# Two spectral filters on one core: the inverse transforms by halves of the columns instead of by branches

## The chip, the cores and the metric

One core of a Trainium2 chip. The metric is device time in microseconds, of the core from start to end of one execution. Engines: TensorE (PE) multiplies matrices into PSUM; VectorE (DVE) and ScalarE (ACT) do elementwise work and move results out of PSUM ("evictions"); SyncE (SP) and GpSimd (POOL) here only issue DMA transfers, which all run on the same 16 DMA engines. Each engine works through its own instruction queue in order and waits on semaphores.

## What is computed

Two branches, A and B, filter the same input `x` (2048 x 1024, bf16) in the frequency domain with different complex weights (2048 x 513), and a gate by row mixes them:

```
g = sigmoid((x * gate_w).sum(-1, keepdims=True))
a = irfft2(rfft2(x) * (A_w_r + 1j * A_w_i)).astype(bf16)
b = irfft2(rfft2(x) * (B_w_r + 1j * B_w_i)).astype(bf16)
return g * a + (1 - g) * b
```

The forward transform is needed once, the product and the inverse twice.

## The kernel before

**The steps.** The 2048-point transform along the rows is split into 128 x 16 points, the 1024-point one along the columns is done by multiplications with cosine and sine tables after folding.

1. `x` comes in 8 transfers. VectorE folds (`fS`, `fT`, for three of eight also `f2`), TensorE does the 128-point transform (`stage_s1`, table F), evictions `Z` write it.
2. `stage_d`: the column transform with table DM, 16 groups of 8 matmuls 128 x 256, evictions `Q`. `stage_s2`: the 16-point transform with table SK, 8 groups of 16 matmuls (64 x 64 tiles, 512 columns), evictions `X` into R4. R4 then holds the spectrum in 16 slots of 2 x 513 elements; four slots are one slot group `sq`.
3. `prod(b, m)`: VectorE multiplies spectrum and weights of branch `b`, two instructions of 2052 elements each, so four for each branch and slot group.
4. `stage_i1(b, m)`: the 16-point inverse of a slot group `sq = m // 2` and half `th = m % 2` of the output rows, 64 matmuls with 64 x 32 tiles and 512 columns (32 wide ones of 64 x 64 in two units). Two evictions `V` of 1024 elements (by ScalarE mostly) bring it to a ring of 28 cells of 512 elements in SBUF.
5. `turn`: a transfer from SBUF to SBUF moves the ring's cells to other partitions, 128 KB each, 64 of them, half on SP and half on POOL. A cell is free again when its turn has landed.
6. `s1inv`: the 128-point inverse for each of 16 row phases n2 and two column kinds c, 8 matmuls 128 x 128 with the gate's tables FM and DM, which sum the two branches (eviction `G`); then `Di`, the column inverse, 4 matmuls 128 x 256 with table DI (eviction `o`). VectorE adds and subtracts (`e`, `y`), SP stores (`out`).

The gate comes from Z (`gate_row`), and `gates`, `gmix` make the tables FM and DM from the table RM (`sig`, `RA`, `RB`).

**The order.** All 16 units of branch A come first, then those of B. While A's products and units run, B's weights arrive: they go to the place where x was (R1), A's to a place of their own (R5). Weights come as rows of 513 elements; one `wpart` transfer is 4 rows for 32 partitions, 128.2 KB (some of A's are twice that), half of them on SP and half on POOL. The tables RM and DI are loaded late, behind given units of B.

**The planner.** Every step is a node with a cost for each engine it may run on. `Plan.run` simulates the engines with these costs and ranks given in RANK and ENGS, places tiles in PSUM banks and ring cells, and writes down the order in which nodes start. `Sched` then fills each engine's queue in that order and adds the semaphore waits. Nothing is reordered on the chip.

The lines that an instruction shows in the profile are mostly those of helpers: L503 every matmul, L506 every elementwise operation of two tensors, L528 ScalarE's and L529 VectorE's evictions, L538 every transfer. They are told apart by tiles and shapes: `R<-R 128x2052` is a product, `64*32 64x512` the 16-point inverse, `DM,R` with 256 columns D, `FM,R` and `DM,R` with 128 columns the 128-point inverse, `DI,RING` Di, `RING<-PS 128x1024` after 46 us V, `R<-RING` a turn.

Of the kernel before, what the change touches and what calls it, by code (L numbers as in the profile page):

```python
# [2 lines left out]

# [10 lines left out]
NS = 513  # L14
# [4 lines left out]
WSPLIT = (((0, 4), (4, 8), (8, 16)), ((0, 4), (4, 8), (8, 12), (12, 16)))  # L19
RANK = (  # L20
    "9v8j0d0e0f0g0h0i0j0k0l0m2z0n0o0p0q0r0s0t0u0v0w0x0y0z1011121314151617191a1c1d1ebacafgey61dzc23u3j3d3p3v4t5r4q4f514j63al5v"
    "4x6s5i7db2686u9q70a7bf6f8vbj95c4bw7g4a7jaucnbkdgbz9s9yaxbledcketc1ewf4fbe6f9enfi3l8h3c6nbp9x7qdyas9mezfcej3a3y54625x6g6c"
    "6v36e33b6a3x3zan4o4z6k6w7275797p82833nef43cu6t6xdu717rcd8acz8od19add9l45eh58eo7u86eq8m8wdtb0dxbee8d7f0dh5jfed5f2c9cfffcm"
    "cq1g1h1i1j1k1l1m1n1o1p1q1r1t1u1v1w1x1y1z212223242527292a2b2c2d2e2f3w46474p37343i39353m3o383t404s4i4d55595g5s5w494k4h564l"
    "4r5a4u4w5b6e5e5p6h64656b6j5d5f6m7b667c7e5q898l7y8b9e8k6l6o6p6r6z8q9n8y8u9r9d789o9w9tara3a67l7n7o7s7vata4awa880b3abb5aj2j"
    "7x818x9088c7b9ccbc98aqb6bm9ccibxd3cb2kbvcjfafh9fdccsdkd49kdmd8drd9aoe5dvege4a9adaz33bhepebereuaeagbyc0c3cwdfdodwe2e7e9fj"
    "fkbdapbue0elei5y2u968t9994f7fl06090003320b02072n043r1s081f4g2l0a2t0501202p1b532m18316d2w263s412g7t3q2o4b7z442q4e280c2r74"
    "2h855o2s4m8d5t2v4v4c3f8f5u2x4y8i5z3057422y5n762i91603e5k977h3h5l525c9i7i3k699z87676y484n777m3ga18p6i73av936q7f7w5hbg9j8c"
    "7kbi9p8n848z507a9ga0bqak8s8ebrb19h8rah8gbtbo9u9bc6cpa2ay925mafb7aic8d0acb4cedbb8bnbsaactdichcod6e1cxcra5bbcgcvamdnevdedj"
    "d2eaecf1dqdpc5clcyfmf3ekf5emdseeexfdf8fof6dldaesfnfp")  # L30
ENGS = (
    "-------------------------------------------------a-a---a-a---a-a---a-a---a-a-----a-a-----a-a-----d-a-a--d--d--a---a-d-d-"
    "a--d-da-da-d-a-d-a--d-da-da-a-d-d-a--a-aa-aa-a-d-a-a--a-aa-aa-------------------------------------a--d---a--d-------a--a"
# [4 lines left out]
UNITS = ((0, 0), (0, 1), (1, 0), (2, 0), (3, 0), (1, 1), (2, 1), (3, 1))  # L38
TD = 3
PAIRS = {"warm": 12, "S2": 16, "I1": 64, "I1w": 32, "S25": 8, "gate": 8, "zg": 4, "gm": 4, "S1i": 8, "S1a": 4, "S1b": 4, "Di": 4}  # L40
WLATE = 1
BLAG = 6
WEARLY = 3
WIDE = 2
# [938 lines left out]
```

## Time and profile before

| | us |
|---|---|
| median of 3 runs | 128.88 (128.09 to 129.44) |
| profiled execution, first to last instruction | 131.6 |
| x load, folding, 128-point transform | 0 to 22.9 |
| D and S2 | 22.9 to about 46 |
| products and 16-point inverse, VectorE full | 46 to 80.4 |
| last units of branch B, gate tables | 80.4 to 96.8 |
| 128-point inverse, Di, outputs | 96.8 to 131.6 |

The profile gives one execution's span, 2.7 us above the median of the runs shown. Its rows are counted from its start. A group's row shows its count, busy time, the mean of one instruction, and the idle time just ahead of it with what ended it; because neighbouring instructions overlap, busy time divided by count is a little less than the mean of one.

### The profile page before, as it was taken

The page shows a single profiled execution, that of the slowest core. Times are in us where ns is not written, and L with a number is a line of the kernel's source. Part 1 is how long each engine was busy: PE and PEld are TensorE (multiplying, and loading weights), DVE is VectorE, ACT ScalarE, POOL GpSimd, SP SyncE. Part 2 cuts the span into 40 slices and gives each one's busy share as a digit, 9 for nine tenths or more (in the row PEclk, how much of TensorE's full clock was granted, in tenths as well). Part 3 has the DMA queues.
Part 4 walks back from the last instruction along what each step waited for, and adds up shares of the span by engine and source line. Part 5 has one row for each costly group of instructions (what it writes and reads, how often), then busy time and mean ns, then how long its engine had stood idle before and what let it go on. Part 6 is the DMA issues. An engine that isn't in the chain of part 4 may idle for free.

```text
span 131.6 us, 4299 instructions
## 1 busy us (share of the span) xinstructions
PE 106.7 (81%) x1844; PEld 72.8 (55%) x1844; DVE 105.3 (80%) x156; ACT 96.5 (73%) x129; POOL 33.8 (26%) x66
## 2 busy tenths in 40 slices
PE   6699995999999797997885640886799999999940
PEld 2288863976777353333332310443369989999820
DVE  1379998487889999999999994024469899999992
ACT  4399998477877997995972922671567869999960
POOL 0000999980000005051441410120334420000000
PEclk9999999999999999999999999599589999999998
DMA  4999999999999999757665890364439560348464
GB/s 99 398 421 413 399 238 240 240 222 194 230 239 235 228 245 234 195 145 210 181 183 173 213 289 24 85 177 149 148 93 263 178 207 0 159 173 345 173 249 183
DMA packets 14021, 27.87 MB, mean 212 GB/s; under 512 B 2577, under 2 KB 8721, under 8 KB 13874
## 3 DMA queue, kind: packets, MB, share of 16 engines
q1 hardware_dynamic: 10720, 19.18, 47.3%
q0 software_dynamic: 3136, 8.40, 25.3%
q8 instruction: 14, 0.23, 0.8%
q14 instruction: 5, 0.04, 0.1%
q10 hardware_dynamic: 146, 0.02, 0.1%
HBM read 15.01 MB, written 4.19 MB: 146 GB/s over the span
## 4 chain that ended last, share of the span: by engine, by line
PE 33%; DMA 26%; DVE 21%; ACT 11%; issue 6%; SPq 1%; DVEq 0%; ACTq 0%; POOL 0%; POOLq 0%
PE PS L503 33%; DMA R<-RING 22%; DVE RING L506 11%; ACT RING L528 7%; DVE R L506 6%; DMA R<-in_A_x_dram 4%; ACT R L528 4%; DVE RING L529 2%; DVE R L529 1%; SPq L538 1%; DVE FM L529 0%; ACT FM L858 0%; DVEq L244 0%; ACTq L244 0%; POOL R L538 0%
## 5 line engine op out<-in xcount | busy, mean ns | idle before, releaser
L528 ACT ACTIVATE RING<-PS 128x1024 bf16<-128x1024 f32 (+1 forms) x62 | 53.4, 920 | 25.7 <-PE PS L503 16.1
L506 DVE TENSOR_TENSOR R<-R 128x2052 bf16<-128x2052 bf16 (+2 forms) x68 | 49.3, 779 | 0.3
L503 PE MATMUL PS<-R,SK 64*32 64x512 bf16 (+1 forms) x960 | 33.5, 409 | 14.1 <-ACT RING L528 11.5
L528 ACT ACTIVATE R<-PS 128x1024 bf16<-128x1024 f32 (+2 forms) x55 | 41.4, 839 | 1.1 <-PE PS L503 1.0
L503 PE MATMUL PS<-DM,R 128*128 128x256 bf16 (+1 forms) x256 | 32.0, 247 | 1.0 <-ACT R L528 1.0
L538 POOL DMA_DIRECT2D R<-RING x32 | 17.3, 541 | 60.0 <-DMA R<-RING 24.0
L503 PEld LDWEIGHTS PS<-R,SK 64*32 64x32 bf16 (+1 forms) x960 | 15.0, 99 | 31.7 <-issue 13.2
L529 DVE CAST RING<-PS 128x1024 bf16<-128x1024 f32 (+1 forms) x18 | 19.2, 1079 | 12.6 <-PE PS L503 12.5
L503 PEld LDWEIGHTS PS<-DM,R 128*128 128x128 bf16 x256 | 25.9, 106 | 3.8 <-ACT R L528 1.5
L506 DVE TENSOR_TENSOR RING<-R 128x1024 bf16<-128x1024 bf16 (+1 forms) x34 | 21.2, 654 | 5.3 <-DMA R<-in_A_x_dram 5.0
L503 PE MATMUL PS<-DI,RING 128*128 128x256 bf16 x128 | 17.2, 273 | 0.3 <-ACT RING L528 0.3
L503 PE MATMUL PS<-FM,R 128*128 128x128 bf16 x128 | 16.5, 219 | 0.2 <-ACT FM L858 0.2
L503 PE MATMUL PS<-R,RING 128*128 128x256 bf16 (+1 forms) x128 | 12.3, 253 | 1.8 <-ACT R L611 1.3
L503 PEld LDWEIGHTS PS<-FM,R 128*128 128x128 bf16 x128 | 12.4, 98 | 1.0 <-ACT FM L858 0.4
L503 PEld LDWEIGHTS PS<-R,RING 128*128 128x128 bf16 x128 | 10.3, 98 | 4.6 <-ACT R L611 1.8
L529 DVE CAST R<-PS 128x512 bf16<-128x512 f32 (+2 forms) x13 | 10.5, 816 | 2.6 <-PE PS L503 2.5
L503 PEld LDWEIGHTS PS<-DI,RING 128*128 128x128 bf16 x128 | 11.5, 98 | 1.7 <-ACT RING L528 0.7
L503 PE MATMUL PS<-RING,SK 64*64 64x512 bf16 (+2 forms) x160 | 9.4, 340 | 1.0 <-ACT R L528 0.6
L538 POOL DMA_DIRECT2D R<-in_A_w_r_dram x6 | 3.6, 600 | 12.4 <-DMA R<-in_A_x_dram 12.4
L503 PEld LDWEIGHTS PS<-RING,SK 64*64 64x64 bf16 (+1 forms) x160 | 3.9, 107 | 4.9 <-ACT R L528 1.3
L538 POOL DMA_DIRECT2D R<-in_B_w_i_dram x9 | 5.6, 634 | 0.0
L538 POOL DMA_DIRECT2D R<-in_B_w_r_dram x8 | 5.2, 646 | 0.0
(30 smaller groups left out, 35.2 us busy)
## 6 DMA issues: line engine op xcount, KB each, us to landing
R<-in_A_x_dram SPq DMA_DIRECT2D x8, 512.0 KB, 7.8
R<-RING SPq DMA_DIRECT2D x32, 128.0 KB, 3.9
R<-RING POOLq DMA_DIRECT2D x32, 128.0 KB, 3.5
out_dram<-RING SPq DMA_DIRECT2D x7, 512.0 KB, 2.6
R<-in_B_w_i_dram SPq DMA_DIRECT2D x8, 128.2 KB, 21.5
R<-in_B_w_r_dram POOLq DMA_DIRECT2D x8, 128.2 KB, 17.1
R<-in_B_w_r_dram SPq DMA_DIRECT2D x7, 128.2 KB, 20.9
R<-in_B_w_i_dram POOLq DMA_DIRECT2D x7, 128.2 KB, 17.8
```

What stands on the lines that cost most here:

```text
L503: return lambda e: e.matmul(o, l, r, start=start, stop=stop, skip_group_check=True)
L506: return lambda e: e.tensor_tensor(out=o, in0=a, in1=b, op=op)
L528: return [lambda e: e.activation(o, i, ACT.Copy)]
L529: return [lambda e: e.tensor_copy(o, i)]
L538: lambda e: [lambda q, d=d, s=s: q.dma_start(d, s) for d, s in pairs()],
```

## The change

**Halves.** The columns 0 to 511 are split in half H (256 to 511, done first) and half L (0 to 255); column 512 is done by itself. A product instruction covers one half, one branch and one slot group, and four slots instead of two (2048 elements). A unit of the 16-point inverse covers one half of *both* branches side by side (512 columns), so the units are named I1H or I1L with slot group and th, as in I1H2.1. Its two V evictions fill two cells each, and one turn moves 256 KB in rows of 1024 elements: 32 turns, TH and TL. Column 512 has four small products (`mul5`), 72 tiny matmuls (`I5`), and 2 matmuls in each L unit that add it with a unit matrix.

**The 128-point inverse of H** (`S1H`, evictions `GH` of 1024 into the place of the used spectrum) needs only H turns and stands between L units in TensorE's queue. Only that of L (`S1L`, `GL`) is left for the end. `Di2` then takes both column kinds, its eviction is 1024 long, `e` too; the last two row phases are done singly (`Di`).

**Places.** Weights of A and B and x share one array, WAB. Products overwrite weights; H's first products stand in the second half of TV, where the L turns land, so L turns wait for the last H unit. `o` and `e` stand in WAB where products of slot groups 0 and 1 were.

**Loads.** RM and DI come early, and weights piece by piece for both branches.

**Order.** The planner is gone: ORDER, ENGS and CELLS hold the order, the engine of each node and the place of each tile, and `replay` reads them. Written out by name, the queues around the change are (WA3.100 is A's weights of slot group 3, odd 1, c 0, J 0; mulH3A0 is half H, slot group 3, branch A, first of two instructions):

```
SP:   x14 F x6 x0 x4 x10 x2 WA3.100 x12 x8 WA2.011 DM WA3.111 WA2.111 WA1.111 WA0.111 DI SK
      WA2.000 WA1.000 WA0.000 RM WA3.000 WA3.011 WA2.100 WA1.011 WA1.100 WB2.100 WB2.011 WB3.111
      WB2.000 WB2.111 WB3.011 WB3.000 WB3.100 WB1.100 WB1.111 WB0.000 WA0.011 WB1.011 WB0.111
      WA0.100 WB1.000 WB0.100 WB0.011 TH2.10 TH2.00 TH3.00 TH3.10 TH1.00 TH1.10 TH0.10 TL2.10
      TL2.00 TH0.00 TL1.10 TL1.00 TL3.10 TL0.10 TL0.00 TL3.00, then the stores
PE:   ... D3.3 D3.2 D2.3 D3.1 D3.0 D2.2 S2.3.1 D2.0 D2.1 gm0 S2.3.0 S2.2.0 S2.2.1 D0.0 D0.1 D0.2
      gm1 D0.3 D1.1 D1.2 S2.0.1 D1.0 D1.3 I1H2.1 I1H2.0 S2.1.1 S2.1.0 I1H3.0 I1H3.1 I5 S2.0.0
      I1L2.1 I1H1.0 I1H1.1 I1L2.0 I1H0.1 I1H0.0 I1L1.1 I1L1.0 I1L3.1 S1H10 S1H14 S1H8 S1H2
      I1L0.1 I1L0.0 S1H4 S1H12 I1L3.0 S1L13 S1L12 S1L10 S1L11 Di2.13 ... S1H0 ... S1H6 ... Di15.0
DVE:  ... Q3.3 Q3.2 Q3.0 X3.11 Q2.1 X3.00 RA0 mulH3A0 X2.11 mulH3A1 Q0.1 mulH2A0 Q0.3 mulH2B0
      mulH2A1 mulH2B1 RB0 RA1 mulH3B0 RB1 mulH3B1 VH2.00 mulL2A0 mulL2B0 mul5 mulL2A1 mul5 mulL2B1
      mul5 mul5 mulH1B0 mulH1A0 mulH1B1 mulH1A1 mulL3A0 mulL3B0 mulH0B0 mulH0A0 mulH0B1 mulH0A1
      mulL1B0 mulL1A0 mulL1B1 mulL1A1 mulL3A1 mulL0B0 mulL3B1 mulL0B1 mulL0A0 VL1.00 VL3.10 mulL0A1
      GH8 GH2 VL0.10 VL0.01 GH12 VL3.00 GL12 o12 e12 ... y15
```

POOL's queue has the other 32 weight transfers and the other 16 turns. The diff, cut to its core:

```diff
-WSPLIT = (((0, 4), (4, 8), (8, 16)), ((0, 4), (4, 8), (8, 12), (12, 16)))
-RANK = (
...
+HL = (256, 0)
+TL = (0, 16384)
+PIECES = ((0, 4), (4, 8), (8, 12), (12, 16))
...
+    def replay(self, order, engs, spots):
...
+            n.eng = names[e]
...
+                    t.at = int(next(spots), 36)
...
+    WAB = sb("WAB", 4 * WH)
+    TV = sb("TV", 32768)
...
+             {"ps": ("ps", 4), "p1": ("ps", 8), "st": ("ring", 4), "q": ("ring", 2), "qx": ("ring", 2), "v": ("ring", 14),
+              "gt": ("ring", 5), "o": ("late", 8), "e": ("late", 8), "y": ("ring", 5), "w": ("ring", 1)})
...
+    cload("sp", RM, 0, "RM", 0, 2048, ["RM"])
...
+    for ci in range(4):
+        for b in range(2):
+            for odd in range(2):
+                for c in range(2):
+                    for J in range(2):
+                        wpart(b, ci, J, odd, c)
+    P.key = ("in", 1)
+    cload("sp", DI, 0, "DI", 0, 2048, ["DI"], more=["xg"])
...
+    def ploc(lh, b, o, cx, s):
+        if o:
+            return WAB, b * 2 * WH + (1 - cx) * WH + s * WP + HL[lh]
+        if lh:
+            return WAB, b * 2 * WH + cx * WH + s * WP + 256
+        return TV, TL[1] + b * 8192 + s * 512 + cx * 256
+
+    def prod(lh, b, sq):
+        P.key = ("P", lh, b, sq)
+        l0 = HL[lh]
+        s0 = 4 * sq
+        x = ap(R4, s0 * 2 * NS + l0, [[2 * NS, 4], [NS, 2], [1, 256]])
+        r = [("X", s0 + i, c, 1 - lh) for i in range(4) for c in range(2)] + wkeys(b, sq)
         for o in range(2):
...
+            P.add("mul", vt(2048), lambda e, w=w, d=d: [tt(d, x, w, ALU.mult)], r, [("P", lh, b, sq, o)], after=old)
...
+                            T, off = ploc(lh, 0, pr // 2, pr % 2, 4 * sq + a + 2 * i)
+                            bs = ploc(lh, 1, pr // 2, pr % 2, 4 * sq + a + 2 * i)[1] - off
...
-                                            rp(b, ps[a], (i * 4 + pr) * NS + c, [[1, 512]], 64 * j, 64), pr == 0, pr == 3))
+                                            ap(T, off, [[bs, 2], [1, 256]], 64 * j, 64), pr == 0, pr == 3))
...
+        old = [("P", 0, b, q, 0) for b in range(2) for q in range(4)] if lh else allz
...
+            ev("V", 1024, lambda j=j: (rg(v[j], 0, [[256, 2], [512, 2], [1, 256]]), psl(t[j], 0, [[512, 2], [256, 2], [1, 256]])),
+               [(t[j],)], [(v[j], 0, 2)], alloc=[v[j]])
+            dma("turn", ("sp", "pool")[j], lambda j=j: [(AP(TV, (64 * j + sq) * pt + TL[lh] + th * 8192, [[4 * pt, 16], [1024, 8], [1, 1024]]),
+                                                         rg(v[j], 0, [[1, 1024]]))], 0.262, 118, [(v[j], 0, 2)], [("V", lh, sq, th, j)], after=old)
...
+    for n2 in range(0, 16, 2):
+        P.key = ("SH", n2)
+        t = Tile("ps", 2)
+        pe("S1H", [128] * 16, lambda n2=n2, t=t: s1inv(0, n2, t, 0) + s1inv(0, n2 + 1, t, 1), vkeys(0, n2), [(t,)], alloc=[t])
+        ev("GH", 1024, lambda n2=n2, t=t: (ap(R4, 2 * n2 * NS + 256, [[NS, 4], [1, 256]]), psl(t, 0, [[256, 4], [1, 256]])),
+           [(t,)], [("GH", n2), ("GH", n2 + 1)], after=[("X", n2 + r, c, 1) for r in range(2) for c in range(2)])
...
+            pe("S1L", [128] * 8, lambda n2=n2, t=t: s1inv(1, n2, t, 0), vkeys(1, n2), [(t,)], alloc=[t])
+            ev("GL", 512, lambda g=g, t=t: (rg(g, 0, [[1, 512]]), psl(t, 0, [[1, 512]])), [(t,)], [(g, 0, 1)], alloc=[g])
...
+                pe("Di2", [256] * 8, both, [(g, 0, 1), ("GH", n2), "DI"], [(t,)], alloc=[t])
+                ev("o", 1024, lambda r=r, t=t: (rg(o, r * 1024, [[1, 1024]]), psl(t, 0, [[1, 1024]])), [(t,)], [(o, 2 * r, 2 * r + 2)],
+                   alloc=[o] if r == 0 else [], after=oldw)
...
+    P.replay(ORDER, ENGS, CELLS)
```

More of the change, by code (lines that the diff above doesn't have):

```diff
@@ L789, in stage_i1 @@
+    def stage_i1(lh, sq, th):
+        P.key = ("I", lh, sq, th)
+        v = [Tile("v", 2), Tile("v", 2)]
         t = [Tile("ps", 2), Tile("ps", 2)]
+        pk = [("P", lh, b, sq, o) for b in range(2) for o in range(2)]
         def fns():
```

532 lines of the change are left out of this document (188 added, 344 removed), and 3 rows, old and new, of the table P.

## The prediction

> **What bounds the kernel now.** I read the table of stretches first, then the chain of waits, then the groups and the transfers. All times are of one profiled execution, counted from its start; its span and its engines' totals:
>
> ```profile
> span 131.6 us, 4299 instructions
> ...
> PE 106.7 (81%) x1844; PEld 72.8 (55%) x1844; DVE 105.3 (80%) x156; ACT 96.5 (73%) x129; POOL 33.8 (26%) x66
> ```
>
> The stretches (busy us and instructions of each engine, granted clock, DMA share, GB/s):
>
> ```profile
> core 0: us, PE busy (x) PEld busy (x) DVE busy (x) ACT busy (x) POOL busy (x), PEclk, DMA share, GB/s
> 22.90:46.10 23.20, 22.24 (x260) 16.58 (x260) 18.89 (x22) 17.63 (x18) 6.36 (x12) 1.00 1.06 227
> 46.10:80.40 34.30, 24.98 (x744) 11.51 (x744) 34.23 (x31) 24.23 (x26) 9.86 (x18) 1.00 0.75 199
> 80.40:96.80 16.40, 11.59 (x272) 5.39 (x273) 4.34 (x7) 7.99 (x10) 2.96 (x6) 0.79 0.39 116
> 96.80:125.20 28.40, 27.94 (x380) 25.75 (x377) 27.43 (x59) 25.85 (x52) 4.43 (x9) 1.00 0.54 185
> 125.20:131.60 6.40, 1.19 (x10) 0.62 (x8) 3.90 (x13) 1.99 (x5) 0.00 (x0) 0.90 0.53 212
> ```
>
> Four stages have four limits. From 22.9 TensorE is full with the forward transforms (D, S2) while the DMA engines are full with weights. From 46.1 VectorE is full with the products (34.23 of 34.30). From 80.4 nothing is full: 16.4 us with VectorE busy for 4.34. From 96.8 three engines are nearly full together. The third stage is the loose one; its rows in the chain (start, us, what), with the last operation, and in the timeline:
>
> ```profile
> 74.45 7.04 DMA R<-RING
> ...
> 128.71 0.42 DVE RING L506
> ```
>
> ```profile
> 81.52 2.85 ACT L528 ACTIVATE RING<-PS 128x1024 bf16<-128x1024 f32 x3 [4.86 <-DMA R<-RING]
> 82.68 5.25 PE L503 MATMUL PS<-R,SK 64*32 64x512 bf16 x128 [5.38 <-ACT RING L528]
> ...
> 88.00 1.23 DVE L529 CAST RING<-PS 128x1024 bf16<-128x1024 f32 x1 [7.64 <-PE PS L503]
> ...
> 88.35 1.93 PE L503 MATMUL PS<-R,SK 64*32 64x512 bf16 x64 [0.42 <-ACT RING L528]
> ...
> 92.94 3.50 PE L503 MATMUL PS<-R,SK 64*32 64x512 bf16 x64 [2.11 <-ACT RING L528]
> ```
>
> A turn issued at 74.45 lands 7.04 us later, ScalarE waits for its buffer, TensorE for ScalarE, and VectorE, out of products, for TensorE. After the idle 5.38 us the granted clock is low, and a 16-point unit of 64 matmuls takes 3.50 where the undisturbed one takes 1.93. The last VectorE operation ends at 129.1; the last store then needs 2.5.
>
> **The change part by part.** By the numbers of operations little goes. Products stay 32 of (now) 2048 elements, plus four of 32. The 16-point inverse stays 16 units. Two of them, of 32 wide matmuls, become 64 narrow ones; and column 512 gets 72 tiny matmuls and 16 additions:
>
> ```profile
> 40.45 0.29 PE L503 MATMUL PS<-RING,SK 128*64 128x2 bf16 x8
> ...
> 46.14 3.96 PE L503 MATMUL PS<-R,SK 64*64 64x512 bf16 x64 [0.86 <-DVE R L506]
> ```
>
> The two wide units take 3.96, 1.98 each, so the 1.93 of a narrow one changes nothing. At 0.29/8 = 0.036 the 72 tiny ones take 2.6 us of TensorE, covered by VectorE's products. 64 turns of 128 KB become 32 of 256 KB, the same bytes. The 128-point inverse keeps its 256 matmuls, of which 96 move ahead of the tail. Evictions there change from 64 of 512 to 22 of 1024 and 20 of 512, the same elements. So the gain can only be in idle time: the 16.4 us stage, which gets the H columns' 128-point inverse as work while turns are under way.
>
> What must be paid is in the loads. Now A's products run while B's weights still arrive; after, the first 16-point unit needs A's and B's weights of slot group 2. Product H2B0 (the fourth mul in VectorE's order) waits for SP's 19th weight transfer, and everything behind it on VectorE waits too. How fast weights come: five issues from the timeline, then the same five among the transfers (KB, us from issue to landing), then the stretch in which x comes:
>
> ```profile
> 6.25 0.58 SPq L538 DMA_DIRECT2D R<-in_A_w_r_dram  x1
> 14.03 0.87 SPq L538 DMA_DIRECT2D R<-in_A_w_i_dram  x1
> 28.56 0.70 POOL L538 DMA_DIRECT2D R<-in_B_w_i_dram  x1
> 30.02 2.22 SPq L538 DMA_DIRECT2D R<-in_B_w_r_dram  x1
> 41.14 1.76 SPq L538 DMA_DIRECT2D R<-in_B_w_i_dram  x1
> ```
>
> ```profile
> R<-in_A_w_r_dram SPq DMA_DIRECT2D x1, 128.2 KB, 12.6
> R<-in_A_w_i_dram SPq DMA_DIRECT2D x1, 256.5 KB, 29.0
> R<-in_B_w_i_dram POOLq DMA_DIRECT2D x1, 128.2 KB, 19.4
> R<-in_B_w_r_dram SPq DMA_DIRECT2D x1, 128.2 KB, 20.9
> R<-in_B_w_i_dram SPq DMA_DIRECT2D x1, 128.2 KB, 14.1
> ```
>
> ```profile
> 8.00:12.00 4.00, 4.00 (x43) 3.39 (x41) 3.94 (x7) 4.00 (x6) 0.00 (x0) 1.00 1.04 420
> ```
>
> On SP the first piece of A lands at 6.25 + 12.6 = 18.85, the last at 14.03 + 29.0 = 43.0. Between them lie 15 pieces of 128.2 KB (A's half on SP is 16), 1.61 us each. POOL's last lands at 28.56 + 19.4 = 48.0. Once POOL's queue is empty SP's go faster: from 50.9 (30.02 + 20.9) to 55.2 (41.14 + 14.1) seven more, 0.61 each. New ahead of the 19th are the tables RM and DI, 0.52 MB each, now loaded early. Their price: at the 420 GB/s of the x loads 2.5 us together, at SP's own share (128.2 KB in 1.61) 12.8. I take 3.8, near the first, because their rows are 4 KB long as those of x are. Until 48.0 SP then lands 1 + (48.0 - 18.85 - 3.8)/1.61 = 16.7 pieces, and the other 2.3 take 1.4: **T0 = 49.4** (48.9 to 52.8 by the ends). VectorE could be there earlier: ahead of it stand 16 of the 24 D and S2 groups that fill 22.9 to 46.1 at 0.97 each, so 38.4, and some evictions, about 41. RM adds a wait of its own: behind SP's ninth piece it lands near 18.85 + 8 x 1.61 + 3.8 = 35.5, while gm0, which reads it and holds the rest of D and S2 behind it on TensorE, is reached at 22.9 + 9 x 0.97 = 31.6. That moves 41 to 45, still before T0. It counts only if the weights come sooner.
>
> From T0 I sum VectorE's queue in its written order, with the durations of these groups (busy time by count, as neighbours overlap):
>
> ```profile
> L506 DVE TENSOR_TENSOR R<-R 128x2052 bf16<-128x2052 bf16 x32 | 36.9, 1220 | 0.0
> L529 DVE CAST R<-PS 128x1024 bf16<-128x1024 f32 x5 | 6.1, 1226 | 2.1 <-PE PS L503 2.0
> L529 DVE CAST RING<-PS 128x512 bf16<-128x512 f32 x6 | 4.1, 685 | 0.1
> L506 DVE TENSOR_TENSOR RING<-R 128x1024 bf16<-128x1024 bf16 x30 | 19.6, 685 | 5.2 <-DMA R<-in_A_x_dram 5.0
> L506 DVE TENSOR_TENSOR R<-R 128x256 bf16<-128x256 bf16 x8 | 1.9, 282 | 0.0
> L506 DVE TENSOR_TENSOR RING<-R 128x512 bf16<-128x512 bf16 x4 | 1.6, 417 | 0.0
> L528 ACT ACTIVATE R<-PS 128x1024 bf16<-128x1024 f32 x27 | 25.9, 1048 | 0.4 <-PE PS L503 0.2
> 42.42 0.19 DVE L529 CAST R<-PS 128x8 bf16<-128x8 f32 x1
> ```
>
> 29 products x 1.153 = 33.4; 10 evictions of 1024 (six V, three GH, one o) x 1.22 = 12.2; 4 of 512 x 0.68 = 2.7; 31 additions and multiplications of 1024 (14 e, 14 y, three for the gates) x 0.653 = 20.2; 8 of 256 x 0.24 = 1.9; 4 of 512 x 0.40 = 1.6; seven tiny ones x 0.19 = 1.3. Together **73.3**. The products read rows of 256 where rows of 513 were read; the additions with inner rows of 256 cost 0.64 ns an element (0.653 by 1024), the products now 0.56 (1.153 by 2052), so a product is between 1.15 and 1.31; I take 1.15, their own row, and keep the 4.4 us for the range.
>
> TensorE starts its first unit at T0 + 3.5 (three products after H2B0) and has 16 x 1.93 = 30.9, 28 for both inverse transforms of the tail (27.94 now), 3 for three S2 and 3 for the tiny ones: 65, so it ends at T0 + 68.5, under VectorE's 73.3. ScalarE has from there 26 V, 6 X, 5 GH and 13 o of 1024 at 0.96 = 48, and 16 of 512 at half that, 56. VectorE is the longest, with little to spare, so it will wait a little: 0.8 for the first unit, which runs at the low clock after TensorE's idle 4 us (1.6 longer, of which VectorE's order covers half), and the 0.97 that it idles in the tail now (28.40 less 27.43). Bounds 0 and 6. I take **1.8**.
>
> Sum: 49.4 + 73.3 + 1.8 + 2.5 = 127.0 of span against 131.6, so 4.6 less. The three runs have a median of 128.88, 2.7 under the profiled span, with a low clock in the profiled one's loose stage; if the 2.7 stays, the time is **124.3**, and if it goes with that stage, 127.0.
>
> **The rivals.**
>
> *Weights in time.* SP and POOL share the engines equally, so SP's piece takes 1.24 instead of 1.61 (the same total of 0.62 a piece). Then the 19th lands at 18.85 + 18 x 1.24 + 3.8 = 45.0, the span is 122.6 and the time **119.9**. Against it stands SP's 1.61. The Trainium skill (DMA: Bandwidth & Descriptors, Queues, rings and completion order) says that each DMA engine takes turns between its queues by packets; if both queues' packets are alike this rival follows. The rows above disagree: SP had 16 pieces landed by 43.0 and POOL all its 32 by 48.0.
>
> *Turns are late.* This one ends slower. V's buffers are used again after two units (VL2.00 takes the cells of VH1.01, VH0.10 those of VH1.11, VL1.10 those of VH0.10). A second wait is added: the L turns overwrite H products and wait for the last H unit, I1H0.0. TL2.10 waits so at SP's head, TH0.00 behind it; POOL does the same. Eight turns then go almost together, 2.1 MB, 7.9 us at the 265 GB/s that 199 at a share of 0.75 (46.1 to 80.4) makes of full engines. The first that need their cells, VL1.01 and VL1.00, come two units (3.9 us) later and the last, VL0.10, four units and 64 matmuls (over 8), so I price this wait at nothing, with VectorE's last products as its cover, and without them at what the eighth is late. The reuse is the tighter loop: four units need two evictions (1.9), the landing, one eviction (0.96) and a unit (1.93), 4.8 + landing, against 8 products (9.2). It decides from a landing of 4.4 us on. Now:
>
> ```profile
> R<-RING SPq DMA_DIRECT2D x32, 128.0 KB, 3.9
> R<-RING POOLq DMA_DIRECT2D x32, 128.0 KB, 3.5
> ```
>
> Twice the bytes in one transfer, but half as many in the queue and in rows twice as long: 3.5 to 5. At the 7.04 of the row above a round takes 11.8, 2.6 more, three rounds from I1L2.1 on 7.9: span 134.9, time **132.2**. The Trainium skill (DMA: Bandwidth & Descriptors, Anatomy of one DMA) gives 2.0 us and the bytes at 436 GB/s, an estimate of 2.6 for 256 KB, by which this rival would be out; the medians of 3.5 and 3.9 for half the bytes are above that.
>
> *The idle time only moves.* VectorE has the same total (105.3 now, 105 by my count); if the wait for weights and the tail, where three engines now share some 24 us each, give back the whole 4.6 us, the time is **128.9**.
>
> **How the numbers follow.** Forecast 0.5 (its own range 122 to 128.5), weights in time 0.2, late turns 0.2, idle time only moved 0.1. 124.3 is the likeliest. The range 118.5 to 131.5 takes in the second case and nearly reaches the third; products at 1.31 are inside it. About 1% is what a measurement of this kernel can tell from no change, 127.6 to 130.2. Faster: 0.43 of the 0.5, 0.19 of the second, 0.62. Same: 0.05, 0.02 of the late turns and 0.07 of the last, 0.14. Slower: 0.02, 0.01, 0.18 and 0.03, 0.24.
>
> **What would show it.** Right: VectorE idle for 4 us or more before its fourth mul, ended by a transfer of B's weights at 48 to 52; then VectorE over 95% busy until 4 us before the end; muls at 1.15; no TensorE wait over 2 us after 60; landings of 256 KB under 4.4. Wrong: a fourth mul before 46 (second case), ScalarE waiting for turns after 60 (third), or VectorE below 90% in the last 28 us (fourth).

## The result and the profile after

The changed kernel takes 142.48 us (median of five runs, 138.91 to 145.58) against 128.67 of the kernel before (128.09 to 129.44): the ratio is 1.087, interval 1.077 to 1.097. It is slower, and 124.3 was forecast.

The ratio, here and below, compares only the faster executions of each kernel (138.91 and 140.42 of the changed one), so it is not the quotient of the two medians, and the profiled execution (here 145.58, the longest of the five, span 143.5) is not always among them. So the order of events is read from this trace, and the prices come from the experiments as well. Its span and totals:

```profile
span 143.5 us, 4504 instructions
...
PE 111.9 (78%) x1996; PEld 76.7 (53%) x1996; DVE 103.6 (72%) x136; ACT 96.9 (68%) x112; POOL 26.8 (19%) x54
```

VectorE's total is about what I counted (103.6; 105 by my sum). So all of the 11.9 us of longer span is time in which VectorE waits. The table of stretches tells where (columns as in the table of before):

```profile
22.90:46.10 23.20, 10.13 (x96) 7.48 (x94) 6.72 (x7) 6.64 (x6) 7.14 (x14) 0.78 1.05 229
46.10:58.20 12.10, 11.50 (x124) 8.00 (x126) 8.80 (x10) 9.44 (x9) 0.00 (x0) 0.86 1.09 221
58.20:93.90 35.70, 30.66 (x953) 15.67 (x952) 35.70 (x40) 30.90 (x36) 5.31 (x10) 1.00 0.55 145
93.90:117.90 24.00, 21.26 (x422) 15.31 (x423) 12.70 (x12) 12.10 (x14) 3.16 (x6) 0.86 0.62 159
117.90:137.10 19.20, 18.27 (x229) 16.62 (x226) 19.02 (x35) 18.95 (x27) 0.00 (x0) 1.00 0.38 151
137.10:143.50 6.40, 0.00 (x0) 0.00 (x0) 3.44 (x9) 0.22 (x1) 0.00 (x0) 0.63 0.52 206
```

Before, TensorE was busy for 22.24 of the 23.2 us from 22.9 to 46.1; now for 10.13. That is the first loss. The stretch between the last product of the long block and the first addition of the outputs (`e`) was 16.4 us with 4.34 of VectorE in it; now it is 24.0 with 12.70. That is the second: VectorE did get 8 us more to do there, and the stretch grew by about as much. Some of it is TensorE's clock: it was granted 0.86 in this stretch, where the base of the later experiments shows 1.00, and behind a wait of 2.78 us a unit took 3.62 us instead of 1.94.

The first loss has two rows in the table of waits, three among the transfers, and these in the timeline (start, us, engine, what; in brackets the idle time ahead and what ended it):

```profile
PE PS L391 <- DMA SK<-c_SK: 11.0, 1, 11.0
...
PE PS L391 <- DMA RM<-c_RM: 2.5, 1, 2.5
```

```profile
DI<-c_DI SPq DMA_DIRECT2D x1, 512.0 KB, 24.7
RM<-c_RM SPq DMA_DIRECT2D x1, 512.0 KB, 32.7
...
SK<-c_SK SPq DMA_DIRECT2D x1, 320.0 KB, 27.8
```

```profile
10.76 0.33 SPq L425 DMA_DIRECT2D DI<-c_DI  x1
11.12 0.43 SPq L425 DMA_DIRECT2D SK<-c_SK  x1
...
13.70 0.58 SPq L425 DMA_DIRECT2D RM<-c_RM  x1
...
39.03 1.92 PE L391 MATMUL PS<-RING,SK 64*64 64x512 bf16 x16 [11.00 <-DMA SK<-c_SK]
...
51.14 1.22 DVE L394 TENSOR_TENSOR TV<-R,WAB 128x2048 bf16<-128x2048 bf16 x1
...
58.17 1.22 DVE L394 TENSOR_TENSOR TV<-R,WAB 128x2048 bf16<-128x2048 bf16 x1
```

SK, which the first S2 group reads, is issued at 11.12 behind six weight transfers and DI and lands 27.8 us later; TensorE stands for 11.0 us, everything of D and S2 behind it. RM lands at 13.70 + 32.7 = 46.4. The first product starts at 51.14 and H2B0, the fourth (58.17), has no wait of its own: VectorE's queue had been held up ahead of it, by TensorE's late D and S2. The weight piece that I made its gate is late too, but covered: issued at 31.43, it lands 24.0 later, at 55.4, and POOL's last piece at 29.41 + 22.3 = 51.7:

```profile
31.43 5.47 SPq L425 DMA_DIRECT2D WAB<-in_B_w_i_dram  x2
```

```profile
29.41 0.63 POOL L425 DMA_DIRECT2D WAB<-in_B_w_r_dram  x1
```

```profile
WAB<-in_B_w_i_dram SPq DMA_DIRECT2D x1, 128.2 KB, 24.0
...
WAB<-in_B_w_r_dram POOLq DMA_DIRECT2D x1, 128.2 KB, 22.3
```

The second loss, from the timeline, and the burst of turns behind it (POOL's four issues in a row, then what was issued from 84 to 92, KB and us to landing):

```profile
85.86 8.07 DVE L394 TENSOR_TENSOR WAB<-R,WAB 128x2048 bf16<-128x2048 bf16 x7
96.17 1.23 DVE L417 CAST RING<-PS 128x1024 bf16<-128x1024 f32 x1 [2.24 <-DMA TV<-RING]
...
117.90 1.29 DVE L394 TENSOR_TENSOR WAB<-WAB 128x1024 bf16<-128x1024 bf16 x2
```

```profile
88.22 2.08 POOL L425 DMA_DIRECT2D TV<-RING  x4 [5.30 <-ACT RING L416]
```

```profile
TV<-RING SPq DMA_DIRECT2D x5, 256.0 KB, 7.5
TV<-RING POOLq DMA_DIRECT2D x4, 256.0 KB, 7.5
```

The long block of products ends at 85.86 + 8.07 = 93.9 (one more, mulL0A1, follows at 100), the first `e` starts at 117.90.

### The profile page after: what moved, and what is told of

Same layout as the page of the kernel before. It is cut to its first block, busy times and chain, and to the rows that moved or that the text cites. A ratio compares the mean times of both kernels' runs of the same rounds, so it can differ in the third digit from the quotient of the medians.

```text
span 143.5 us, 4504 instructions
## 1 busy us (share of the span) xinstructions
PE 111.9 (78%) x1996; PEld 76.7 (53%) x1996; DVE 103.6 (72%) x136; ACT 96.9 (68%) x112; POOL 26.8 (19%) x54
## 4 chain that ended last, share of the span: by engine, by line
DMA 39%; PE 22%; DVE 18%; ACT 13%; SPq 3%; issue 2%; ACTq 0%
DMA RM<-c_RM 23%; PE PS L391 22%; DMA TV<-RING 11%; ACT RING L416 10%; DVE RING L394 7%; DVE WAB L394 6%; DMA WAB<-in_A_x_dram 5%; SPq L425 3%; ACT R L416 3%; DVE RING L417 2%; DVE R L417 1%; DVE WAB L417 1%; ACTq L247 0%
## 5 line engine op out<-in xcount | busy, mean ns | idle before, releaser
L416 ACT ACTIVATE RING<-PS 128x1024 bf16<-128x1024 f32 (+1 forms) x48 | 45.0, 988 | 18.4 <-PE PS L391 11.9
L391 PE MATMUL PS<-DM,TV 128*128 128x256 bf16 (+1 forms) x256 | 33.2, 256 | 0.5 <-DMA DM<-c_DM 0.4
L391 PE MATMUL PS<-WAB,SK 64*32 64x512 bf16 x768 | 25.6, 397 | 3.7 <-ACT RING L416 2.8
L391 PEld LDWEIGHTS PS<-DM,TV 128*128 128x128 bf16 x256 | 26.6, 109 | 3.1 <-ACT TV L416 0.8
L394 DVE TENSOR_TENSOR WAB<-R,WAB 128x2048 bf16<-128x2048 bf16 x24 | 28.1, 1227 | 0.0
L416 ACT ACTIVATE R<-PS 128x1024 bf16<-128x1024 f32 (+1 forms) x21 | 18.0, 914 | 14.1 <-PE PS L391 14.1
L394 DVE TENSOR_TENSOR RING<-WAB 128x1024 bf16<-128x1024 bf16 (+1 forms) x34 | 21.3, 655 | 3.9 <-DMA WAB<-in_A_x_dram 3.6
L391 PE MATMUL PS<-RING,SK 64*64 64x512 bf16 (+2 forms) x160 | 11.3, 401 | 12.1 <-DMA SK<-c_SK 11.0
L391 PE MATMUL PS<-FM,TV 128*128 128x128 bf16 x128 | 16.7, 227 | 1.4 <-DMA TV<-RING 1.4
L416 ACT ACTIVATE WAB<-PS 128x1024 bf16<-128x1024 f32 (+1 forms) x17 | 15.1, 945 | 1.2 <-PE PS L391 1.1
L391 PE MATMUL PS<-DI,R 128*128 128x256 bf16 x64 | 14.6, 273 | 0.0
L416 ACT ACTIVATE TV<-PS 128x1024 bf16<-128x1024 f32 x14 | 13.4, 1042 | 0.2
(46 smaller groups left out, 94.6 us busy)
```

The source lines that it names most:

```text
L391: return lambda e: e.matmul(o, l, r, start=start, stop=stop, skip_group_check=True)
L394: return lambda e: e.tensor_tensor(out=o, in0=a, in1=b, op=op)
L416: return [lambda e: e.activation(o, i, ACT.Copy)]
```

## The experiments

All ratios are to the kernel before on the same chip, with a 95% interval. The kernels ran in five groups on several chips. The kernel before took 131.48 us in the first group and 128.84 in the last, on the same chip, so a difference of 0.01 to 0.02 between ratios of different groups decides nothing; the traces' times from H2B0 on serve beside them. Each kernel moves steps in the written order by a small helper: `move(pick, behind)` takes the steps that `pick` names and puts them behind the last one that `behind` names; each engine's queue and all semaphore waits follow from the new order.

**The loads (three kernels of one chip).** The first moves the tables, the second the weights, the third both.

```
move(c_SK, c_RM  -> behind c_DM);  move(c_DI -> behind the last weight)        # tables
move(W12, W13 -> behind fS, fT, W02, W03);  move(W00, W01, W10, W11 -> behind W12, W13)   # weights
```

The names W02 to W13 are branch (0 is A, 1 is B) and slot group: the second edit loads the slot groups 2 and 3 of A, then of B, ahead of 0 and 1.

> SK and RM issued right behind DM on SP, DI behind the last weight; nothing else. In the changed kernel SK lands at 38.9 us with TensorE idle 11.0 for it, RM at 46.4 with 2.5 more, and the last product ends 13.5 later than in the kernel before (93.9 against 80.4). Theory 'tables' (these two waits are the loss): about 13 us come back, 129.5 us. Theory 'weights' (B's weights of slot group 2 arrive at 54.5 anyhow, which the late tables now hide, so the fourth product moves from 58.2 to 52 or 54 at best): 4 to 6 us come back, 137 to 138.

> Only the order of the weights on SP and POOL: slot groups 2 and 3 of A and B first, groups 0 and 1 behind them; the tables stay where the change has them. Theory 'tables': TensorE still waits for SK to about 39 and for RM to about 46, so 142.5 us as in the changed kernel, within 1.5. Theory 'weights' as sole cause: the fourth product comes sooner, 137 us. If both waits lie side by side: 142.5, as the tables still bind.

> Tables as in the first and weights as in the second. Theory 'tables': nothing beyond the first run, 129.5 us in both. Theory 'weights': 6 to 8 us below the first run, 129 to 131, because only together do they let the first 16-point unit start at about 47 to 49 instead of 61.8.

Measured: tables 1.062 (1.052 to 1.072; 139.16 us), weights 1.050 (1.041 to 1.059; 139.45), both 1.036 (1.027 to 1.044; 136.50), with 131.48 before on that chip. With the tables moved TensorE's waits for SK and RM are gone, and the first product now waits for A's weights; with both moved, H2B0 waits for B's. The first fence is of the kernel with the tables moved, the second of the one with both, the third a row of waits of the one with the weights moved.

```profile
45.42 1.23 DVE L394 TENSOR_TENSOR TV<-R,WAB 128x2048 bf16<-128x2048 bf16 x1 [9.13 <-DMA WAB<-in_A_w_i_dram]
```

```profile
48.66 1.23 DVE L394 TENSOR_TENSOR TV<-R,WAB 128x2048 bf16<-128x2048 bf16 x1 [3.31 <-DMA WAB<-in_B_w_i_dram]
...
83.32 4.66 DVE L394 TENSOR_TENSOR WAB<-R,WAB 128x2048 bf16<-128x2048 bf16 x4 [1.10 <-PE PS L391]
...
108.53 1.29 DVE L394 TENSOR_TENSOR WAB<-WAB 128x1024 bf16<-128x1024 bf16 x2
```

```profile
PE PS L391 <- DMA SK<-c_SK: 3.7, 1, 3.7
```

"Tables" as the only cause falls: it expected 129.5 from the first edit, which took 139.16. "Weights" expected the fourth product at 52 to 54 there, and it starts at 53.23. The second edit does not part the two: it leaves four pieces instead of six ahead of SK and five instead of nine ahead of RM, so the tables come earlier too, and TensorE waits 3.7 us for SK instead of 11.0 and none for RM. Behind TensorE's wait for SK and RM lies one for A's weights, which I hadn't looked at in the new order, and behind that one for B's; the two edits together take 5.1 of the 8.7% away, by the ratios. They bring H2B0 to 48.66, about where I had put it, though other pieces stand ahead of it there. But the span is then 134.1 and not 127: from H2B0 to the end it takes 85.4 us, of which 20.6 are the stretch (88.0 to 108.5), where the forecast had 73.3 + 1.8 + 2.5 = 77.6. That part of the loss is no load's.

**The hold of the L turns.** An L turn overwrites H products, so it waits for the last H unit while its cells of the ring stay taken. All four kernels have both loads moved. The first (in the group of the three above) writes H's first products over weights that the second products still read, so that L turns needn't wait; the second also moves L2's four turns right behind their evictions; the third keeps the reference's output and puts all H steps ahead of all L steps on every engine, with cells given anew; the fourth only gives the cells anew.

```
-                d, old = ap(TV, ploc(0, b, 0, 0, s0)[1], [[512, 4], [256, 2], [1, 256]]), allf
+                d, old = w, []                                      # no hold
+ move(turns of L2, th -> behind the V of L2, th)                    # + early turns
+ move(L products, units, V, turns that stand ahead -> behind the last H step)   # all H first
+ t.at = min(free, key=lambda s: (max(c[s:s + t.n]), s))             # cells: longest free first
```

> As the third, and half H's first products are written in place over the weights (so they overwrite what the second products read, and the output is not the reference's), so that no L turn has to wait for the last H unit. Same instructions, same bytes. Theory 'held turns' (eight turns of 256 KB let go together at 88 us in the changed kernel, landing after up to 7.5 us, are what keeps the late stage idle): 4 to 7 us below the third run, 122 to 126. Rival 'order' (the late stage is limited by the sequence of units, evictions and turns, 512 KB for each unit at some 240 GB/s, however early a turn starts): within 1.5 us of the third run.

> H's first products are written over weights as in the run without the hold of the L turns (the output is not the reference's), the loads stand as in the run with both moves, and the four turns of L2 also stand right behind the evictions that they read in both queues, so that they go out some 8 us earlier (there POOL sent TL2.11 only with the burst of four at 80.08). Theory 'held turns' (L2's turns keep eight cells of the ring until the last H unit, and eight turns then go together): the burst is gone, ScalarE's wait of 3.72 and VectorE's of 4.64 for turns at 84 to 88 fall under 1 each, and from the end of the products (83.6 there) to the first e addition it takes 17 to 19 instead of 26: span 127 to 130, ratio to the kernel before 0.99 to 1.01 (1.048 there). Theory 'bandwidth' (the late stage is as long as its turns need at some 240 GB/s): the waits move to later turns, ratio 1.035 or more.

> The loads stand as in the run with both moves; besides, all products, units, evictions and turns of the H columns stand ahead of those of the L columns on every engine and queue, and the cells of the ring and of PSUM are given anew to this order, the cell that has been free longest first. The output is the reference's. L turns then find their places free when they are made. Theory 'held turns': no burst of eight turns at 83.5, from H2B0 to the end 78 to 81 us instead of 85.4, ratio 0.99 to 1.01 (1.036 there). Theory 'bandwidth': the same bytes in the same stretch, ratio within 0.01 of 1.036. Theory 'reuse of cells': gains here and as much in the run that only gives the cells anew.

> The loads and the order stand as in the run with both moves; only the cells of the ring and of PSUM are given anew, the cell that has been free longest first, instead of by the recorded list. Theory 'reuse of cells': ScalarE's and VectorE's waits for turns (0.76, 1.89, 1.77 at 79 to 90) go, 2 to 4 us less, ratio 1.005 to 1.02. Theories 'held turns' and 'bandwidth': the ring has 28 cells and the held turns still keep theirs, so within 0.01 of 1.036.

Measured: no hold 1.048 (1.040 to 1.055); with early turns 1.056 (1.042 to 1.070); cells anew 1.048 (1.037 to 1.058), 134.91 us, span 132.4; all H first 139.91 us (136.36 to 143.74) against 129.28, which gave no interval, but the shortest of its four runs is above the longest of the kernel before (131.40). None is clearly better than the kernel with both loads moved: in the same group, no hold has 1.048 for 1.036, and from H2B0 to the end cells anew takes 85.0 us for 85.4. Yet the waits that the theories named did go: with all H first and with cells anew VectorE and ScalarE wait for no turn any more. With all H first the stretch even fell to 16.9 us (91.1 to 108.1), but VectorE waits 5.7 us, in two waits, for the last spectrum ahead of H's products, and from H2B0 to the end it is 87.0. TensorE has no idle time in those 16.9 us. So the hold and the reuse of cells, as the cause of the lost 8 us, fall. In the kernel with cells anew the stretch is still 72.48 + 12.62 = 85.1 to 105.02, 19.9 us:

```profile
72.48 12.62 DVE L394 TENSOR_TENSOR WAB<-R,WAB 128x2048 bf16<-128x2048 bf16 x11
...
105.02 1.29 DVE L394 TENSOR_TENSOR WAB<-WAB 128x1024 bf16<-128x1024 bf16 x2
```

It is the base of the runs that follow.

**What fills the stretch.** TensorE has work in it (five L units, six groups of H's 128-point inverse, the first of L's), and the turns travel in it. One edit for each:

```
-                   rg(v[j], 0, [[1, 1024]]))], 0.262, 118, ...
+                   rg(v[j], 0, [[1, 512]]))], 0.131, 118, ...        # half turns (and [1, 512] at the target)
-                for b in range(2):      +                for b in range(1):   # half of the 128-point inverse
+ move(mulL0A1 -> behind mulL0A0); move(S1H/GH 10, 4, 2, 14, 8 -> into the tail)   # TensorE's work later
```

> The loads stand as in the run with both moves; each of the 32 turns moves 128 KB instead of 256, the first half of every row (the second half is left out, so the output is not the reference's). Theory 'bandwidth': landings fall from 5.1 and 4.5 to about 3, the waits for turns between 78 and 105 go, 5 to 8 us less, ratio 0.98 to 1.00. Theory 'held turns': the burst still goes at 83.5, but with half the bytes it lands in 4.5 instead of 8, so 3 to 4 us less, ratio 1.005 to 1.015. If neither (order of the engines' queues alone): within 0.01 of 1.036.

> As the run with the cells given anew (1.0475 to the kernel before on its chip; H2B0 at 47.4, last product of the block 85.1, first e addition 105.0, span 132.4). In addition the last product mulL0A1 stands right behind mulL0A0 on VectorE, and five of the six S1H groups that TensorE has ahead of the last L units (10, 4, 2, 14, 8, with their evictions) stand in the tail, each just ahead of the direct transform that reads it; S1H12 stays. Theory 'TensorE's rest' (when VectorE's products end, TensorE has some 20 us left that must come before the first e addition, and it is full in 85 to 105): 5 x 0.92 = 4.6 us leave that stretch, the first e addition comes 3.5 to 4.6 us earlier, the tail (24.5 us, VectorE full, TensorE 3 to 5 us of slack) takes 0 to 1.5 of it back: span 128.5 to 130, ratio 1.015 to 1.03. Theory 'transport' (the first e addition waits for the landing of TL0.1x and TensorE's work only fills that wait): TensorE stands idle ahead of S1L13 instead, ratio 1.04 to 1.05.

> As e9, with turns that move 128 KB instead of 256 (the second half of each row is left out, so the output is not the reference's). In the order of the changed kernel this was worth about 0.01 to 0.02 (1.026 against 1.036 and 1.0475). Theory 'TensorE's rest': worth no more here, within 0.015 of e9, as TensorE is still full until the first e addition. Theory 'transport': with TensorE's filling gone the landings are the path, and half the bytes are worth 3 us or more, 0.025.

> Base is the run with the cells given anew (1.0475; H2B0 47.4, first unit 51.06, products end 85.1, first e addition 105.0, TensorE's last matmul 125.1, span 132.4). Here the 128-point inverse of both column halves sums one term instead of two (128 of its 256 matmuls are left out, so the output is not the reference's): TensorE has 7 us less to do after the first unit, all else is as it was. Theory 'TensorE's path' (from the first unit on TensorE has 67 of 74 us full, and VectorE waits for it in 85 to 105): 4 to 6.5 us less, ratio 1.00 to 1.015. Theory 'VectorE's queue' (73 us from H2B0, as I predicted): under 1.5 less, 1.035 to 1.05. Theory 'transport': between products and first e under 1 us less, the tail 1 to 2, ratio 1.03 to 1.04.

> Base is the run with the cells given anew (span 132.4, products end 85.1, first e addition 105.0). Here both cuts together: half the terms of the 128-point inverse (7 us of TensorE) and turns of 128 KB (the output is not the reference's). Each alone left the stretch between the last product of the block and the first e addition at about 20 us. Theory 'side by side' (TensorE's work and the transport, that of the turns and of TensorE's code, both need about 20 us there, and whichever is left stands): 14 to 16 us now, first e addition at 99 to 101, with the tail of 22.5 of the run with TensorE's cut a span of 125 to 127.5, ratio 0.98 to 1.00. If a chain of waits from unit to unit sets it, independent of both: 19 to 20 again, span 130 to 131.5, ratio 1.015 to 1.03.

Measured, with the stretch from the last product of the block to the first `e`, and the time from H2B0 to the end of the span:

| kernel | ratio or us | stretch | us | H2B0 to end |
|---|---|---|---|---|
| cells anew (base) | 1.048 (1.037 to 1.058) | 85.1 to 105.0 | 19.9 | 85.0 |
| both loads moved (base of the next row) | 1.036 (1.027 to 1.044) | 88.0 to 108.5 | 20.6 | 85.4 |
| half turns, cells as recorded | 1.026 (1.015 to 1.037) | 85.9 to 105.8 | 20.0 | 83.4 |
| half of the 128-point inverse | 1.027 (1.012 to 1.041) | 84.4 to 106.0 | 21.6 | 84.6 |
| TensorE's work later | 1.117 (1.098 to 1.137) | 88.2 to 109.2 | 21.0 | 94.6 |
| work later and half turns | 1.083 (1.076 to 1.090) | 87.1 to 102.1 | 15.1 | 87.7 |
| half inverse and half turns | 128.86 (127.85 to 129.18), before 128.84 (126.59 to 129.90) | 84.9 to 100.9 | 16.0 | 79.3 |

Neither cut alone shortens the stretch; both together take 4 to 5 us off it (in the two kernels with the work later one product fewer stands in it). The first row below is of the kernel with half the inverse, the second of the one with both cuts:

```profile
106.00 1.29 DVE L394 TENSOR_TENSOR WAB<-WAB 128x1024 bf16<-128x1024 bf16 x2
```

```profile
72.29 12.63 DVE L394 TENSOR_TENSOR WAB<-R,WAB 128x2048 bf16<-128x2048 bf16 x11
...
100.91 1.29 DVE L394 TENSOR_TENSOR WAB<-WAB 128x1024 bf16<-128x1024 bf16 x2
```

The table of stretches shows the two lying side by side. It has two halves of the stretch each for the base, for half turns and for half the inverse, and the first ten us for both cuts, whose stretch ends at 100.9 (behind the window and its length the first column is TensorE; the last two are the transfers' share and GB/s):

```profile
85.10:95.10 10.00, 8.31 (x213) 5.88 (x220) 6.65 (x7) 3.88 (x5) 1.05 (x2) 1.00 0.94 256
95.10:105.10 10.00, 10.00 (x211) 7.88 (x188) 6.11 (x7) 6.25 (x9) 1.58 (x3) 1.00 0.58 162
```

```profile
85.10:95.10 10.00, 8.34 (x222) 5.74 (x206) 6.73 (x6) 4.80 (x5) 1.58 (x3) 1.00 0.39 110
95.10:105.10 10.00, 10.00 (x221) 7.63 (x221) 6.00 (x6) 6.48 (x8) 1.58 (x3) 1.00 0.30 82
```

```profile
85.10:95.10 10.00, 5.82 (x157) 3.41 (x146) 5.50 (x5) 3.54 (x4) 1.47 (x3) 1.00 0.94 236
95.10:105.10 10.00, 9.05 (x209) 5.98 (x194) 5.77 (x6) 6.48 (x8) 1.58 (x3) 1.00 0.54 146
```

```profile
85.10:95.10 10.00, 8.77 (x238) 5.29 (x230) 9.06 (x8) 5.83 (x6) 1.80 (x4) 1.00 0.32 89
```

In the base TensorE has 18.3 of 20 us and the transfers 0.94 of the first ten. With half turns the share falls to 0.39 and TensorE keeps its 18.3: nothing is won. With half the inverse TensorE falls to 14.9, the share stays at 0.94: nothing is won either. "Side by side" is shown in this sense, that a cut of one gains nothing in the stretch and a cut of both does; a chain of waits independent of both falls (it expected 19 to 20 for both cuts), and so do "TensorE's path" and "transport" as the only cause. By the ratios alone half turns are worth 3% with the work moved and 1 to 2% without, where the intervals touch; half the inverse may be worth 2%, through the tail, which is 22.6 us instead of 24.5. Its 1.027 lies in none of the three ranges expected, and the 1.026 of half turns is nearest to the case in which neither bandwidth nor the hold counts.

How the turns hold the stretch up when TensorE has less to do, the waits of the run with half the inverse tell. TensorE is idle there for 5.2 of the 21.6 us. None of this is a wait for a turn; 3.2 us are two stops (2.46 and 0.76) without a wait that the profile shows. The longer one:

```profile
87.82 1.68 PE L391 MATMUL PS<-WAB,SK 64*32 64x512 bf16 x49 [2.46 <-issue]
```

With both cuts TensorE is idle for 1.9 of 16.0 us and has no such stop in the stretch. VectorE's idle time in the stretch is ended by TensorE in every kernel of the table with cells given anew. So TensorE is what the stretch goes by; in the kernels where it has less to do there while turns of 256 KB travel, it is held up in its own queue.

Why the move of TensorE's work into the tail cost 7% instead of giving 2% shows in two places. The larger is the tail: from the first `e` to the last VectorE operation it grew from 24.5 to 30.7 us, as it had no room on TensorE. The other is in the stretch. The L units then follow each other without a pause, six turns issued within 5.3 us land after 9.2 and 9.6 us in the median, and TensorE stops in the middle of a unit, after 10 of its 64 matmuls, without a wait that the profile shows:

```profile
TV<-RING SPq DMA_DIRECT2D x3, 256.0 KB, 9.6
TV<-RING POOLq DMA_DIRECT2D x3, 256.0 KB, 9.2
```

```profile
96.11 3.05 PE L391 MATMUL PS<-WAB,SK 64*32 64x512 bf16 x54 [4.06 <-issue]
```

In that stop, at 93.3, a 16 KB transfer of the instruction queue is recorded, so late code for TensorE fits the row: the profile counts these transfers among those of the same 16 engines, whose share is 1.06 in the stop. The places of the stops speak for it too. Counted in the traces' records, the nine stops of over 2 us in the experiments lie behind 598, 726, 1363 or 1490 matmuls of TensorE's queue (within one), a multiple of some 127.5 apart. They don't go with a given step of the kernel: with 14 matmuls put in ahead (`warm2`, below) the stop still lies behind 598, and so in another step. That the stop is the code's is thus well supported, but no edit tried it by itself. The Trainium skill (Runtime: NRT & Kernel Launch, Instruction fetch mechanics) says that code comes in blocks of 16 KiB by the sequencer's own DMA queue and that crossing a boundary is mostly hidden. The changed kernel's trace agrees on the blocks (15 transfers, 0.25 MB); if the stop is the code's, by its 4.06 us it isn't hidden while turns fill the engines.

**The tail, and the clock.** One kernel does the e and y operations on half of their columns and leaves the other half out. Another has 14 matmuls that nobody reads ahead of the first unit, where TensorE idles 3.7 us and the first unit runs at a low clock (0.54 granted from 51 to 54 in the base, 1.91 us for its first 32 matmuls).

```
- ... [[512, m], [1, 256]]) ... [d, [256, 2], [1, 256]] ...
+ ... [[512, m], [1, 128]]) ... [d, [256, 2], [1, 128]] ...          # half of e and y
+ pe("warm2", [512] * 14, lambda: [mm(psl(wt, 0, [[1, 512]]), ap(SK, 0, [[1, 128]]), ap(SK, 0, [[1, 512]]), True, True) ...
```

> Base as in the run with half the 128-point inverse. Here the e and y operations on VectorE work on half of their columns (28 of 0.65 us become 0.40, the other half is left out, so the output is not the reference's): VectorE has 7 us less in the tail, TensorE the same. Theory 'VectorE's queue': 5.5 to 7 us less, ratio 0.99 to 1.005. Theory 'TensorE's path': only the 4.4 us that VectorE needs behind TensorE's last matmul and a few waits shrink, 1.5 to 3 us less, ratio 1.025 to 1.035.

> Base as before. Here 14 matmuls of 512 columns on a table, whose result nobody reads, stand between the last forward transform and the first unit, where TensorE waits 3.7 us; in the base the first unit then runs at a low clock (32 matmuls in 1.91, 1.56 and later 1.91 again instead of 1.06). Theory 'clock': 1.06 for each 32 from the first unit on, 1.3 to 2 us earlier there, and by 'TensorE's path' 1 to 2 us less in the whole, ratio 1.03 to 1.04. If VectorE's products cover it: products end at 85 all the same, and the whole within 0.01 of 1.0475.

Measured: half of e and y 134.93 us (132.12 to 137.90) against 130.30, no interval; in its trace the tail is 105.67 to 127.4, 21.7 instead of 24.5, with TensorE's last matmul at 124.9 (125.4 in the base). 7 us less work for VectorE shorten it by 2.8, so TensorE sets the tail but for its end. Warming gave 1.040 (1.021 to 1.058), not told apart from the base. The first unit did run in 1.06 for each 32 matmuls, but a stop of 3.05 us of the kind above came at the place in the queue where the base stops for 1.06, and the products ended at 87.1. What the clock costs stays open.

**The weights shared out anew.** On top of the work moved into the tail, three of B's pieces go from SP to POOL and three back.

```
+ move(WB2.111, WB3.000, WB3.100 -> POOL, behind its last piece of groups 2 and 3)
+ move(WB0.001, WB1.010, WB1.001 -> SP, behind the last weight)
```

> As e9, and three of B's pieces of slot groups 2 and 3 (WB2.111, WB3.000, WB3.100) go from SP's queue to POOL's and three of B's groups 0 and 1 from POOL's to SP's, so that the pieces needed first end on both queues at about the same time. By SP's 1.61 and POOL's 1.0 us a piece H2B0's last weights land at 42 to 43 instead of 47.2. Theory 'weights': VectorE waits for TensorE's transforms instead (D and S2 end at 47), H2B0 at 44 to 45, 2 to 3.4 us less than e9. Theory 'one total': the engines are full at 243 GB/s from 30 to 60, so the wait moves to another piece and the gain is under 1.

Measured 1.126 (1.109 to 1.144), not told apart from 1.117 without it. H2B0 starts at 47.09 instead of 48.21, now waiting 2.05 for another of B's pieces. In the other experiments with the loads and products placed alike it starts at 46.85 to 48.66, so 1.1 us is no gain that can be told from chance. This fits "one total" (with full engines the last piece needed comes when all are in); the 2 to 3.4 us of "weights" are not there.

## Why the prediction was wrong

The work itself was priced about rightly: VectorE's total was 103.6 for 105, and a product of 2048 elements takes 28.1/24 = 1.17 (1.15 taken). By the terms of the sum, H2B0 started at 58.17 instead of 49.4 (+8.8), VectorE's work from there took 70.9 instead of 73.3 (-2.4), its waits 11.5 instead of 1.8 (+9.7), and the end 2.9 instead of 2.5: 143.5 for 127.0. So two steps failed, the price of the loads and one comparison of totals.

**The loads.** H2B0's weights were to land at 49.4 and landed at 55.4, and TensorE was later still. The mis-sized term is that of the tables: "I take 3.8, near the first, because their rows are 4 KB long as those of x are" is for RM and DI together, and SK, behind six weights and DI, had no price at all, though TensorE needs it before RM. The landings in SP's queue show what each took behind the transfer ahead of it. The sixth and the ninth piece (issued at 9.11 and 12.76):

```profile
WAB<-in_A_w_i_dram SPq DMA_DIRECT2D x1, 128.2 KB, 22.5
...
WAB<-in_A_w_r_dram SPq DMA_DIRECT2D x1, 128.2 KB, 29.8
```

The sixth lands at 31.6, DI at 35.4, SK at 38.9, the ninth at 42.6, RM at 46.4. So DI took 3.8, SK 3.5 and RM 3.8, together 11.1 where 3.8 stood in the sum. Near x's rate was wrong for them, but SP's own share (12.8 for RM and DI) was too much: these two took 7.6. DM, which now also stands behind two pieces, took 4.7 more. "RM adds a wait of its own: behind SP's ninth piece it lands near 18.85 + 8 x 1.61 + 3.8 = 35.5" fails by the same terms: it landed at 46.4, and TensorE had by then stood for 11.0 us for SK. Besides, POOL's last piece landed at 51.7 instead of 48.0; by then 13 of SP's were there, and the other six took 3.7 us. The range for T0 (to 52.8) left SK out and so ended too low.

**The stretch after the products.** "TensorE starts its first unit at T0 + 3.5 [...] 65, so it ends at T0 + 68.5, under VectorE's 73.3" compares two totals. In the base of the later runs the first unit starts at T0 + 3.7 as forecast, but TensorE's last matmul ends at T0 + 78.0, since of its work 18.3 us (the two rows of the base above) stand behind VectorE's last product of the block and ahead of the first `e`, where VectorE's queue has little but V and GH evictions. So the step that failed is "VectorE is the longest": the two engines' lists stand partly one behind the other. In the sum, the 1.8 us of VectorE's waits were the mis-sized term: in the changed kernel 58.17 to 140.6 is 82.4 us with 35.70 + 12.70 + 19.02 + 3.44 = 70.9 of work and 11.5 of waits, 11.3 of them from 93.9 to 117.9. The bounds that I gave, 0 and 6, didn't hold it either.

**The rivals.** "Turns are late" named the burst of eight turns and the ring as the place, and its threshold (a landing of 4.4) was reached on POOL (4.7) and nearly on SP (4.2). But its mechanism is not the cause: without the hold, or with cells that are free in time, nothing is won. The turns count beside TensorE's work, by what they do to TensorE when they fill the engines. "The idle time only moves" is what happened in kind: the 16.4 us stretch came back as 17 to 27 in the kernels with all the work, in most as 20 to 24. "Weights in time" falls. Of the signs that would show it right, VectorE's wait before the fourth mul is seen only once the tables are moved; of those that would show it wrong, two came: ScalarE waited 6.1 us for turns, and VectorE was busy for 85% of the last 28 us.

No version here beats the kernel before. Of those with the reference's output the lowest ratio is 1.036, with both loads moved; 1.040 and 1.048 are not told apart from it. The one with both cuts comes near the kernel before (equal medians, but its shortest run is 127.85 for 126.59), so the order would be at best about level if TensorE and the turns had less to do there. A larger ring was not tried.

## What to carry to other kernels

A stage with idle engines is not filled by totals: list for each engine what stands between the last operation of one stage and the first of the next, and take the longest of these lists, transfers included. When two such lists are equally long, an experiment that shortens one shows nothing; cut both before you call either harmless. When an order of loads is written anew, look at every small table in the queue and not only at the large pieces, and ask which engine stops first if it is late.

## What the runs showed of the hardware

- A table behind weight pieces pays more than its bytes at x's rate. With POOL's weights under way, 512 KB in SP's queue took 3.8 us (DI, RM) and 320 KB 3.5 (SK) behind the transfer ahead; in the kernel before, where POOL's first piece landed only at 19.6, SK's 288 KB took 1.4 (DM landed at 16.5, SK at 17.9), and x came at 420 GB/s.
- 32 turns of 256 KB land after 4.2 to 4.7 us in the median, but four or five close together on each queue after 7.5, and six issued within 5.3 us after 9.2 to 9.6; the engines then show a share near 1 at 230 to 256 GB/s, where x comes from DRAM at 420.
- TensorE can stop for 2 to 4 us without a wait that the profile shows, in the middle of a step. The kernel before and the changed kernel as given have no such row; of the fifteen experiments seven have nine stops of 2.0 to 4.1 us. The transfers' share is 0.97 to 1.06 in eight of them and 0.69 in one, and each has a 16 KB transfer of the instruction queue that starts between 0.8 us before it and 1.2 us after its start.
